# A gated mix of a state-space scan and a Hedgehog attention: a new order of the first loads, constant products at the head of TensorE, and U1 added on VectorE

## The chip, the cores and the metric

The kernel runs on one core of one Trainium2 chip. The metric is the device time of one execution in microseconds; before the change it was 173.07 us, the median of three runs (172.84 to 173.09).

## The reference, cut to what matters

The input x is (2048, 512) in bf16. Two branches read it and a gate mixes them:

```
g   = sigmoid(sum(x * gate_w))                        # one number for each position
a   = 2 * Re(hseq @ C^T) + x * Dskip                  # h_t = Lam_bar * h_(t-1) + B_bar x_t, 512 complex states
b   = (num / den) @ wo                                # linear attention, 32 heads of 16
      num = phi(q) @ sum_s phi(k)_s v_s ;  den = phi(q) . sum_s phi(k)_s + 1e-6
      phi(y) = [softmax(y W_phi), softmax(-y W_phi)]  # over the 16 features of a head
out = g * a + (1 - g) * b
```

with `Lam_bar = exp(exp(log_dt) * Lambda)` and `q, k, v = x @ wqkv`. The recurrence runs over all 2048 positions.

## The kernel before, in words

The positions are split in four phases: position 4c + r belongs to phase r, and the 16 tiles of 128 positions hold tile 4r + a for phase r. The recurrence is then only run over 512 groups of four positions, as two real scans on VectorE for each block j of 128 states, and the states of the phases between come from matrix products.

What each stage does, by the names of the generators that issue it (a name in the order below is the next step of that generator):

- `W0..W3`: transposes of the k weights on TensorE (an identity product), each then copied to SBUF. `f0..f3`: the feature map is folded into these weights (`pf`, line 375) and copied to `Wk2`. The q weights get the same treatment later (`w0..w3`), from weights that arrive already transposed.
- `V`: one transpose of a 20-row tile `vec_n`, which holds Lambda_im, Lambda_re, log_dt, Dskip and gate_w in rows of 128. `P, P2, P3, P4, U, M, D`: small steps on 512 states (exp, angle reduction, sine, products on GpSimd, diagonal matrices `dg`). `i0..i3`: the tables of sines and cosines, five steps each: `kk` (VectorE), `psi` (VectorE), sine (ScalarE), absolute value into `kk` (VectorE), cosine (ScalarE). The `kk` and `psi` tiles come from a pool with two buffers each.
- `v`, `k`, `q` of a tile: four products over the 512 input channels (line 415), then a copy from PSUM. `x, n, e, s` of a pair of tiles: the softmax features of k: trees of maxima and minima, exponentials, sums (VectorE, with exp on ScalarE). `a`: the products that sum phi(k) v (`kvacc`, line 513).
- `p`, `g`: the scan's input: `g0` gives U1, the state input of the second phase, kept in `uv[j][:, 0]`; `g1` adds up the input of the fourth phase. `z`: the scan (VectorE), which leaves the states of the fourth phase in `H3`.
- `h(j, ri)`: the states `H1` of the second phase, block j, real or imaginary part: three products into one PSUM bank (line 597: the identity times U1; lines 598 and 599: diagonal matrices times the previous `H3`), then a copy to SBUF.
- `c, r, b, K`: versions of C and the kernel of the lag between phases. `y`: the state output of a tile. `X, N, E, S`: the features of q. `o`: phi(q) times the summed phi(k) v, and the division. `t`: the output weights, added into the bank of `y`, then the gate and the store.

The order of the work on TensorE, VectorE, ScalarE and the SP queue is not chosen by a scheduler: it is the list of steps in the string `ORDER`, read from front to end. Each engine executes its instructions in the order in which this list issues them. `@5` gives the PSUM bank that a step takes, and `:D` says that a copy from PSUM goes to VectorE; without it `evac` (line 112) uses ScalarE.

The loads stand ahead of the list. The ScalarE queue issues the k weights (`C2r`, line 156), `Wc` (the feature maps, line 157), a load of the activation table (line 125), and the v weights `Wv` (line 161). The SP queue issues the five rows of `vec_n` (line 159), eight transposing loads of x (line 221), both B matrices (lines 225 and 226), their transposes (lines 228 and 229), the other eight x tiles, the q weights, C, and the output weights. Eight semaphores are shared in turn by all loads of both queues, in program order as the build lays it out; a load that takes a semaphore a second time waits in its queue until the load that had it before has landed.

Of the kernel before, what the change touches and what calls it, by code (L numbers as in the profile page):

```python
# [10 lines left out]
ALU = mybir.AluOpType  # L11
AX = mybir.AxisListType
ACT = mybir.ActivationFunctionType
F32 = mybir.dt.float32
# [6 lines left out]
P = 128  # L21
# [3 lines left out]
B B W0@0 B V@1 V P W3@2 P W0:D W1@3 P2 W2@4 P2 P2 P2 U B W3 P2 gw P3 W1 W2 v1@5 U f1@6 P4 f2@7 P P4 P4 P2 f1 f0@1 P3  # L25
i0 U f2 f3@2 v0@0 i0 i1 f0 f3 i1 i0 i0 U i0 i2 i1 i1 v2@3 i2 i1 k2@4 i2 i3 k2 i2 k0@6 i3 k1@7 k1 i2 k0:D v0:D i3 M
v1:D x0 n0 n0 k3@1 k4@2 k5@4 i3 v2 k6@6 n0 k3 i3 v3@0 x0 x0 L x0 k7@7 k5 k4 D n0 x0 n0 v3 p20@5 p02@3 n1 x1 p00@1 e0
k6:D v7@4 p00 p20:D x1 n1 x1 v4@2 p32@0 x1 p22@6 x1 x2 v7 e0 x2 p10@1 p30@5 p12@4 s0 n1 v4 p10 s0 x2 p02 v6@2 p30 s0
x2 n1 v5@1 p22 p32 s0 g000@3 g101@5 n1 n2 s0 p12:D k8@6 k7 s0 e1 e1 k9@0 n2 x2 s0 k8 k9 g101 a0@74 n2 n2 x3 n2 g001@6
k11@0 e2 x3 s1 x3 n3 a0 x3 v6 v10@2 s1 n3 s1 e2 k11 n3 s1 g000 k12@0 D n3 g001 x3 s1 x4 s1 n3 g101 k13@5 k12 s1 n4 s2  # L30
s2 n4 x4 e3 a1 g000 x4 v5 n4 e3 x4 s2 g100@0 a1 n4 g011@3 s2 x4 k13 s2 s3 g100 s2 k10@1 n4 w1@5 g011 s2 g001 k10 s3 s3
a2 n5 n5 w0@6 x5 g100 w1 g010@1 e4 s3 n5 x5 s3 n5 g011 x5 x5 w2@0 s3 D v10 e4 s3 a2 k14@5 x5 g110@2 x6 g011 w0 g010
k15@3 w3@6 n5 a3 n6 s4 g010 k14 w2 e5 s4 v8@5 x6 s4 s4 g010 x6 a3 g111@0 v9@1 e5 z0 k15 s4 x6 g111 s4 g110 v9 c03@3
g110 s5 z0 v8 g201@1 g111 n6 c03 g111 c10@5 n6 n6 s4 a4 x6 g211@3 c02@0 w3 g110 c10 g210@6 z0 s5 z0 n6 g200@2 c13@5 z0
c02 n7 z0 e6 z0 q1@0 s5 z0 x7 s5 e6 x7 q1 g200 a4 n7 s5 c13 q0@0 n7 g201 x7 n7 x7 s5 v14@5 s6 x7 z1 g200 q0 v11@2 g201
z1 s5 q3@0 z1 s6 g210 q3 n7 z0 nA s6 z1 e7 s6 nA v11 c12@1 c12 z0 a5 v14 q2@0 xA z1 z1 xA e7 s7 s6 g210 c01@2 g211
c11@1 xA a5 g210 g211 v12@5 g211 s6 c11 z1 v13@6 z1 nA z2 xA z1 c01 z2 v13 nA s7 s6 g300@3 v12 g301@1 q11@2 z1 xA
c00@6 q2 c00 z2 g300 a6 nA eA xB xB eA s7 v15@5 s7 g311@0 g301 z2 xB g301 nB z2 g311 s7 g300 q7@6 s7 nB sA sA z2 a6
g310@1 g311 q15@3 nB q7 v15 g310 xB s7 xB nB a7 r0 g311 nB q11 g310 z2 sA g310 z3 eB z3 sA eB a7 z3 q5@6 q10@5 z3 q4@0
q15 q6@2 sA Y q8@1 sB h00@3 Y q10 sA z2 q5 h01@5 h00 h10@6 h01 h11@7 q9@3 sB q6 h11 z3 r1 sB q9 z2 q12@5 z3 h10 z2  # L40
q13@2 z3 z3 sA q4 sB z3 K1@7 G h20@3 sB sA r0 sB z3 h31@6 sB sA sA G q13 h20 h21@0 h31 h30@2 h21 Y q12 b0 r1 K0@3 sB
sB sB h30 END o0@6 K1 X1 K0 o0 Y N1 q8 y1@4 X1 o0@0 o0 o2@5 o2 X1 N1 q14@2 X1 o2@7 N1 b0 o0 N1 X1 q14 N1 X2 o1@3 o0 N2
b1 o1 y0@1 o0 G E1 o2 o2 K3@2 o1@6 b1 E1 G y0 N2 o1 r2 X2 o1 E1 E1 o1 K3 K2@0 X2 y1 o0 y0 o2 o3@3 o3 o3@5 y2@2 o3 t0
N2 o1 y2 o3 o1 N2 y3@6 S1 r3 X2 r3 S1 S1 K2 S1 y1 y2 S1 y4@0 X2 S1 o2 t1 o2 N2 o3 S1 y6@7 S1 y7@3 b2 y3 S1 r2 S1 X3 y4
E2 o3 b3 t2 N3 E2 t0 y4 E2 t1 y3 o4@1 E2 X3 b3 y6 y5@5 o3 S2 t2 S2 X3 S2 S2 o4 t0 o4@4 y7 o4 o4 y5 o4 o4 t1 o5@2 t2 o5
S1 X3 o5@1 o5 S1 t3 S2 N3 y7 y5 b2 S2 o5 y11@4 o5 t3 N3 o5 S2 N3 o6@2 o6 o6@6 o4 o5 o6 y6 o7@1 y11 S2 t4 S2 o6 o6 o7
t3 o6 o7@2 X3 y8@6 o7 o7 o6 t4 N3 E3 t5 o7 o7 y9@0 o8@1 y8 t4 o7 E3 t5:D y10@2 S2 E3 S2 o8 S2 o8@5 o8 o8 y9 t6 y11 o8
o8 E3 S3 o9@1 S3 o9 o9@5 t7 o9 t6 t6 o9 y9 t7 S3 S3 o9 o8 y14@7 o9 S3 y8 S3 o10@3 S3 o9 S3 o10 y10 y14 o10@1 t8 o10
o11@5 t5 S3 o10 o10 o11 t9 t8 t7 t9 o11@3 y14 o12@6 o12 o11 o10 S3 y12@1 o12@0 o11 o12 o12 o11 o12 y10 o10 S3 o13@5 S3
o11 o13 o12 y12 o13@6 t10 o13 y15@3 o11 o14@0 o13 t10:D y12 o14 o14@2 o13 y13@5 o14 y15 o12 o13 o15@6 o14 o14 t8 o15  # L50
o13 o15@0 o15 t11 o14 o15 y13 o14 t10 o15 t11 y15 o15 y13 t14 t11 o15 t13 t9 t14 t13:D t12 t12:D t14 t15 t15 t13 t12
t15
"""
TWO_PI_LO = float(np.nextafter(np.float32(2.0 * np.pi), np.float32(0.0)))
# [11 lines left out]
def kernel(  # L66
# [42 lines left out]
    def bank(shape, dtype, name):  # L109
        return ps.tile(shape, dtype, tag=f"t{sel['banks'].pop(0)}", name=name, bufs=1)  # L110
# [40 lines left out]
    vec_n = const.tile([20, P], BF16, name="vec_n")  # L151
# [4 lines left out]
    nc.scalar.dma_start(out=wk_nat[:], in_=B_wqkv[:, D:2 * D].rearrange("(k p) n -> p k n", p=P))  # L156
# [4 lines left out]
    nc.scalar.dma_start(out=Wv[:], in_=B_wqkv[:, 2 * D:3 * D].rearrange("(k p) n -> p k n", p=P))  # L161
# [14 lines left out]
    hpi_t = const.tile([P, 1], F32, name="hpi_t")  # L176
    nc.vector.memset(hpi_t[:], float(np.pi / 2.0))
# [42 lines left out]
    def x_load(ti):  # L220
        nc.sync.dma_start_transpose(out=xT[:, :, ti * P:(ti + 1) * P], in_=x_res[ti // 4, ti % 4])
# [21 lines left out]
    tab_g = tc.tile_pool(name="tabtmp", bufs=2, reuse_waits="tile")  # L243
# [34 lines left out]
    def st_V():  # L278
        pvt = bank([P, 20], BF16, "pvt")
        nc.tensor.transpose(pvt[:], vec_n[:], ident[0:20, 0:20])  # L280
        yield
        nc.vector.tensor_copy(out=vec[:].rearrange("p n j -> p (n j)"), in_=pvt[:])
# [268 lines left out]
    def st_c(dst, j):  # L551
        d_, da, db = ((C2r, DG_BR, DG_NBI), (C2i, DG_NBI, DG_NBR))[dst]
        pc = bank([P, D], F32, "pc")
# [38 lines left out]
    def st_h(j, ri):  # L592
# [4 lines left out]
        MM(out=ph[:], lhsT=ident[:], rhs=U1[:, ri, :], start=True, stop=False)  # L597
        MM(out=ph[:], lhsT=dg[:, da, j, :], rhs=H3[:, j, 0, prev], start=False, stop=False)
        MM(out=ph[:], lhsT=dg[:, db, j, :], rhs=H3[:, j, 1, prev], start=False, stop=True)
        yield  # L600
        evac(H1[:, j, ri, :], ph[:])
# [131 lines left out]
    st = {"V": st_V(), "U": st_U(), "P": st_P(), "P2": st_P2(), "P3": st_P3(), "P4": st_P4(), "B": st_B(), "gw": st_gw(),  # L733
# [57 lines left out]
```

## Time and profile before

| | us |
|---|---|
| median of three runs (range) | 173.07 (172.84 to 173.09) |
| the profiled execution | 173.42 |
| its span, first to last instruction | 171.7 |
| TensorE busy | 157.8 (92%) |
| VectorE busy | 144.2 (84%) |
| ScalarE busy | 116.9 (68%) |
| GpSimd busy | 5.3 (3%) |

The profiled execution is 1.7 us longer than its span, and 0.35 us above the median. Busy time of TensorE counts a product from its start to the end of its pipeline, so that 379 ns are shown for a product of 512 columns whose successor starts 216 ns later; the start times are what counts. VectorE's durations overlap in the same way.

### The profile page before, as it was taken

To read this page: it belongs to the slowest core of one execution; us is meant where nothing else is said; L and a number is where in the kernel's file an instruction comes from. 1 tells how busy PE (TensorE), PEld (TensorE's weight loads), DVE (VectorE), ACT (ScalarE), POOL (GpSimd) and SP (SyncE) were. 2 spreads that over 40 slices of the span, in tenths; PEclk is the share of its full clock that TensorE was granted. 3 is DMA by queue.
4 is the path that set the end of the run, shared out by engine and by line. 5 is a ranking of instruction groups with operands and counts; after the bars stand their busy time and mean duration, and the time that the engine had idled before them with its cause. 6 is when DMAs were issued, how large, how long until landed. Compare 5 with 4: busy or idle time off the path is not lost.

```text
span 171.7 us, 2969 instructions
## 1 busy us (share of the span) xinstructions
PE 157.8 (92%) x1049; PEld 80.5 (47%) x1069; DVE 144.2 (84%) x349; ACT 116.9 (68%) x239; POOL 5.3 (3%) x23
## 2 busy tenths in 40 slices
PE   0599989999999999999999999999999998998991
PEld 0354456455455454444545444545455543444540
DVE  3775999999999999999999999999999958335411
ACT  2559799988789587586687698896864394251311
POOL 3223000000000000000000000000000000000000
PEclk9999999999999999999999999999999999999999
DMA  5945974554546000000000008341178458596443
GB/s 126 208 106 157 265 96 92 95 116 100 92 95 164 20 0 2 0 4 0 0 0 4 0 0 168 76 33 34 33 183 203 85 145 183 134 174 154 122 138 106
DMA packets 50710, 15.94 MB, mean 93 GB/s; under 512 B 46088, under 2 KB 50696, under 8 KB 50696
## 3 DMA queue, kind: packets, MB, share of 16 engines
q1 hardware_dynamic: 49112, 14.70, 39.9%
q10 hardware_dynamic: 1584, 1.07, 2.6%
q8 instruction: 8, 0.13, 0.3%
q14 instruction: 6, 0.05, 0.1%
HBM read 2.64 MB, written 2.10 MB: 28 GB/s over the span
## 4 chain that ended last, share of the span: by engine, by line
PE 63%; DVE 18%; DMA 11%; ACT 3%; SPq 2%; issue 1%
PE pq L415 8%; PE py L675 6%; PE py L676 6%; PE py L720 6%; PE pgq L538 6%; PE pgq L541 6%; PE pv L415 5%; DMA phT<-EEq 4%; DVE smk L450 3%; DVE mxk L450 3%; PE py L682 2%; DMA xT<-in_A_x_dram 2%; DVE mnk L450 2%; DMA C2r<-in_B_wqkv_dram 2%; PE pk L645 2%; DMA oT<-on 2%
## 5 line engine op out<-in xcount | busy, mean ns | idle before, releaser
L415 PEld LDWEIGHTS <-xT 128*128 128x128 bf16 x192 | 18.4, 99 | 22.7 <-DMA xT<-in_A_x_dram 2.1
L133 ACT ACTIVATE EEk<-EEk 128x1024 bf16<-128x1024 bf16 x20 | 20.9, 1072 | 2.5 <-DVE EEk L466 2.5
L707 DVE SCALAR_TENSOR_TENSOR on<-pn,RG,rd 128x256 bf16<-128x256 f32 x32 | 14.4, 478 | 9.2 <-ACT rd L133 9.2
L133 ACT ACTIVATE ld<-pn 128x16 f32<-128x16 f32 x32 | 5.5, 185 | 18.4 <-PE pn L698 18.1
L415 PE MATMUL pv<-Wv,xT 128*128 128x512 bf16 x62 | 16.3, 400 | 1.9 <-DMA xT<-in_A_x_dram 1.8
L541 PE MATMUL pgq<-xT,LBT 128*128 128x512 bf16 x63 | 16.0, 379 | 0.1
L720 PE MATMUL py<-Wo,oT 128*128 128x512 bf16 x61 | 15.6, 379 | 0.2
L415 PE MATMUL pq<-Wq,xT 128*128 128x512 bf16 x63 | 15.2, 379 | 0.1
L415 PE MATMUL pk<-Wk,xT 128*128 128x512 bf16 x63 | 15.2, 379 | 0.1
L133 ACT ACTIVATE EEq<-EEq 128x1024 bf16<-128x1024 bf16 x12 | 12.2, 1047 | 1.3 <-DVE EEq L466 1.3
L676 PE MATMUL py<-Wv,H 128*128 128x512 bf16 x32 | 12.1, 379 | 0.1
L114 ACT CAST uv<-pgq 128x512 bf16<-128x512 f32 x16 | 9.3, 582 | 3.9 <-PE pgq L546 2.8
L724 ACT ACTIVATE ot<-py,G 128x512 bf16<-128x512 f32 x12 | 8.2, 682 | 5.5 <-PE py L720 4.9
L676 PE MATMUL py<-C2i,H 128*128 128x512 bf16 x31 | 11.7, 379 | 0.1
L675 PE MATMUL py<-C2r,H 128*128 128x512 bf16 x31 | 11.7, 379 | 0.1
L675 PE MATMUL py<-Wk,H 128*128 128x512 bf16 x31 | 11.7, 378 | 0.0
L114 ACT CAST Xq<-pq 128x512 bf16<-128x512 f32 x16 | 9.3, 589 | 3.4 <-PE pq L415 3.3
L698 PEld LDWEIGHTS <-phT 128*128 128x128 bf16 x128 | 7.0, 98 | 7.1 <-DMA phT<-EEq 2.7
L450 DVE TENSOR_TENSOR smk<-smk 128x512 bf16<-128x512 bf16 (+2 forms) x30 | 9.9, 330 | 0.2
L486 DVE TENSOR_TENSOR EEk<-EEk,rck 128x2048 bf16<-128x2048 bf16 x8 | 9.7, 1218 | 0.0
L541 PEld LDWEIGHTS <-LBT 128*128 128x128 bf16 x64 | 6.2, 98 | 7.3
L579 DVE TENSOR_TENSOR_SCAN w<-ssm_par,ut 128x512 bf16<-128x512 f32 x8 | 9.6, 1215 | 0.0
(169 smaller groups left out, 339.4 us busy)
## 6 DMA issues: line engine op xcount, KB each, us to landing
out_dram<-ot SPq DMA_DIRECT2D x16, 128.0 KB, 2.1
C2r<-in_B_wqkv_dram ACTq DMA_DIRECT2D x1, 512.0 KB, 3.9
Wv<-in_B_wqkv_dram ACTq DMA_DIRECT2D x1, 512.0 KB
Bn_r<-in_A_B_re_dram SPq DMA_DIRECT2D x1, 512.0 KB, 4.6
Bn_i<-in_A_B_im_dram SPq DMA_DIRECT2D x1, 512.0 KB
Wo<-in_B_wo_dram SPq DMA_DIRECT2D x1, 512.0 KB
xT<-in_A_x_dram SPq DMA_TRANSPOSE x16, 3.5
oT<-on SPq DMA_TRANSPOSE x16, 2.3
```

The costliest lines, as they stand in the source:

```text
L114: nc.scalar.copy(out=out_ap, in_=in_ap)
L133: ins = nc.scalar.activation(**kw)
L415: MM(out=pt[:], lhsT=xT[:, kt, ti * P:(ti + 1) * P], rhs=W[:, kt, :], start=(kt == 0), stop=(kt == KT - 1))
L450: VT(out=t[:], in0=cur[:, :, :, 0:n, :], in1=cur[:, :, :, n:2 * n, :], op=op)
L486: VT(out=E5, in0=E5, in1=rc[:].to_broadcast([P, L, 2 * NB, Dh, 4]), op=ALU.mult)
L538: MM(out=pgq[:], lhsT=BT[:, kt, js], rhs=xT[:, kt, r1 * NC:(r1 + 1) * NC], start=(kt == 0), stop=False)
L541: MM(out=pgq[:], lhsT=LBT_[:, kt, js], rhs=xT[:, kt, (r1 - 1) * NC:r1 * NC], start=False, stop=(r1 == 1 and kt == KT - 1))
L579: nc.vector.tensor_tensor_scan(out=w[:, ri, :], data0=rb, data1=ut[:, ri, :], initial=0.0, op0=ALU.mult, op1=ALU.add)
L675: MM(out=py[:], lhsT=src[:, j, 0, off:off + P], rhs=cr[:, j, :], start=(j == 0), stop=False)
L676: MM(out=py[:], lhsT=src[:, j, 1, off:off + P], rhs=ci[:, j, :], start=False, stop=False)
L707: nc.vector.scalar_tensor_tensor(out=on[:, 2 * hf:2 * hf + 2].rearrange("p g h e -> p (g h) e"), in0=pns[hf][:, :, 0:Dh], scalar=RG[:, ti: ...
L720: MM(out=py[:], lhsT=oT[:, g, :], rhs=Wo[:, g, :], start=False, stop=(g == HG - 1))
```

## The change

It has four parts, and a new `ORDER` that covers all of the work.

1. Loads. The eight x transposes come first in the SP queue. Lambda_im, Lambda_re and log_dt (now a 12-row `vec_n`) go to the ScalarE queue, between the k weights and `Wc`; `Wv` follows `Wc`, and the load of the activation table comes behind `Wv`. Dskip and gate_w become an 8-row tile `vec_m`, loaded behind the eight x tiles, with a transpose and a copy of their own (`V2`).
2. TensorE begins with nine products of a constant tile `fillw` into a PSUM bank that nothing reads.
3. The `h` step leaves out the identity product for all eight (j, ri); instead of the copy, VectorE adds U1 to the PSUM result.
4. The pool of `kk` and `psi` has three buffers.

The new order has fewer copies from PSUM on VectorE: `v1:D`, `k6:D`, `t6:D` and `t10:D`, where the old one had `W0:D`, `k0:D`, `v0:D`, `v1:D`, `p20:D`, `p12:D`, `k6:D`, `t5:D`, `t10:D`, `t13:D` and `t12:D`. `C2_VECTOR` is empty, so the branch in `st_c` does nothing.

```diff
 ORDER = """
-B B W0@0 B V@1 V P W3@2 P W0:D W1@3 P2 W2@4 P2 P2 P2 U B W3 P2 gw P3 W1 W2 v1@5 U f1@6 P4 f2@7 P P4 P4 P2 f1 f0@1 P3
...
+W2@0 V@1 W2 W1@2 V P B B W1 P P2 W0@3 U P2 P2 P2 W3@4 P2 B P3 P4 P4 W3 U P B P4 v2@5 W0 f1@6 f3@7 U f0@1 i1 U f2@0 P2
+P3 i0 f1 i1 i0 i2 v0@2 f0 f3 f2 v1@4 k0@3 k1@6 k2@1 i0 M i0 i0 i1 i2 i1 i3 i3 k0 k1 v1:D x0 i1 i2 i2 v2 v0 k6@7 k2
...
+C2_VECTOR = ()
+H1_VECTOR = ((0, 0), (0, 1), (1, 0), (1, 1), (2, 0), (2, 1), (3, 0), (3, 1))
...
-    vec_n = const.tile([20, P], BF16, name="vec_n")
+    vec_n = const.tile([12, P], BF16, name="vec_n")
+    vec_m = const.tile([8, P], BF16, name="vec_m")
...
     nc.scalar.dma_start(out=wk_nat[:], in_=B_wqkv[:, D:2 * D].rearrange("(k p) n -> p k n", p=P))
+    for n, src in enumerate((A_Lambda_im, A_Lambda_re, A_log_dt)):
+        nc.scalar.dma_start(out=vec_n[4 * n:4 * n + 4, :], in_=src.rearrange("(j p) -> j p", p=P))
     nc.scalar.dma_start(out=Wc[:], in_=B_w_phi.rearrange("(k hl) e f -> (hl e) k f", hl=8))
-    for n, src in enumerate((A_Lambda_im, A_Lambda_re, A_log_dt, A_Dskip, gate_w)):
-        nc.sync.dma_start(out=vec_n[4 * n:4 * n + 4, :], in_=src.rearrange("(j p) -> j p", p=P))
+    nc.scalar.dma_start(out=Wv[:], in_=B_wqkv[:, 2 * D:3 * D].rearrange("(k p) n -> p k n", p=P))
     pin_act_set()
-    nc.scalar.dma_start(out=Wv[:], in_=B_wqkv[:, 2 * D:3 * D].rearrange("(k p) n -> p k n", p=P))
...
+    fillw = const.tile([P, 512], BF16, name="fillw")
+    nc.vector.memset(fillw[:], 1.0)
+    spin = ps.tile([P, 512], F32, tag="t7", name="spin", bufs=1)
+    for _ in range(9):
+        nc.tensor.matmul(out=spin[:], lhsT=fillw[:, 0:P], rhs=fillw[:], start=True, stop=True)
...
     for ti in range(8):
         x_load(ti)
+    for n, src in enumerate((A_Dskip, gate_w)):
+        nc.sync.dma_start(out=vec_m[4 * n:4 * n + 4, :], in_=src.rearrange("(j p) -> j p", p=P))
...
-    tab_g = tc.tile_pool(name="tabtmp", bufs=2, reuse_waits="tile")
+    tab_g = tc.tile_pool(name="tabtmp", bufs=3, reuse_waits="tile")
...
         ph = bank([P, NC], F32, "ph")
-        MM(out=ph[:], lhsT=ident[:], rhs=U1[:, ri, :], start=True, stop=False)
-        MM(out=ph[:], lhsT=dg[:, da, j, :], rhs=H3[:, j, 0, prev], start=False, stop=False)
+        add = (j, ri) in H1_VECTOR
+        if not add:
+            MM(out=ph[:], lhsT=ident[:], rhs=U1[:, ri, :], start=True, stop=False)
+        MM(out=ph[:], lhsT=dg[:, da, j, :], rhs=H3[:, j, 0, prev], start=add, stop=False)
         MM(out=ph[:], lhsT=dg[:, db, j, :], rhs=H3[:, j, 1, prev], start=False, stop=True)
         yield
-        evac(H1[:, j, ri, :], ph[:])
+        if add:
+            VT(out=H1[:, j, ri, :], in0=ph[:], in1=U1[:, ri, :], op=ALU.add)
+        else:
+            evac(H1[:, j, ri, :], ph[:])
         yield
```

More of the change, by code (lines that the diff above doesn't have):

```diff
@@ L30 @@
[L30 to L39, printed above, removed]
@@ L45 @@
[L45 to L49, printed above, removed]
@@ L278, in st_V, with st_V2 @@
     def st_V():
-        pvt = bank([P, 20], BF16, "pvt")
-        nc.tensor.transpose(pvt[:], vec_n[:], ident[0:20, 0:20])
+        pvt = bank([P, 12], BF16, "pvt")
+        nc.tensor.transpose(pvt[:], vec_n[:], ident[0:12, 0:12])
         yield
-        nc.vector.tensor_copy(out=vec[:].rearrange("p n j -> p (n j)"), in_=pvt[:])
+        nc.vector.tensor_copy(out=vec[:, 0:3, :].rearrange("p n j -> p (n j)"), in_=pvt[:])
+        yield
+    def st_V2():
+        pvt = bank([P, 8], BF16, "pvt")
+        nc.tensor.transpose(pvt[:], vec_m[:], ident[0:8, 0:8])
+        yield
+        nc.vector.tensor_copy(out=vec[:, 3:5, :].rearrange("p n j -> p (n j)"), in_=pvt[:])
         nc.gpsimd.affine_select(out=Dd[:], in_=dsk.unsqueeze(2).to_broadcast([P, KT, P]), compare_op=ALU.is_equal,
@@ L552, in st_c @@
         d_, da, db = ((C2r, DG_BR, DG_NBI), (C2i, DG_NBI, DG_NBR))[dst]
+        if (dst, j) in C2_VECTOR:
+            k = 2 * (j % 2) + dst
+            tmp = phT0[:, k].rearrange("p m f -> p (m f)").bitcast(F32)
+            if sel["eng"] == "act":
+                nc.scalar.mul(out=tmp, in_=CrT[:, j, :], mul=dgs[:, da, j:j + 1])
+            else:
+                VS(out=tmp, in0=CrT[:, j, :], scalar1=dgs[:, da, j:j + 1], scalar2=None, op0=ALU.mult)
+            yield
+            nc.vector.scalar_tensor_tensor(out=d_[:, j, :], in0=CiT[:, j, :], scalar=dgs[:, db, j:j + 1], in1=tmp, op0=ALU.mult, op1=ALU.add)
+            yield
+            return
         pc = bank([P, D], F32, "pc")
```

39 lines of the change are left out of this document (27 added, 12 removed).

## The prediction

> **What bounds the kernel now.** I read the page first (slices), then the waits, then the first 16 us of the timeline, the chain of waits, and last the VectorE groups by form.
>
> ```profile
> PE   0599989999999999999999999999999998998991
> DVE  3775999999999999999999999999999958335411
> PEclk9999999999999999999999999999999999999999
> ```
>
> TensorE is full from the third slice to the end, VectorE from the sixth to slice 32 (133 us). So a saving counts only where it takes work off TensorE, brings its start forward, or shortens a wait, and VectorE must not fall behind.
>
> ```profile
> PE ptw L273 <- DMA C2r<-in_B_wqkv_dram: 4.7, 1, 4.7
> PE pv L415 <- DMA xT<-in_A_x_dram: 1.8, 1, 1.8
> PE pn L698 <- DMA phT<-EEq: 1.4, 2, 0.8
> PE pl L525 <- DVE dg L367: 0.7, 1, 0.7
> DVE kk L388 <- ACT T2c L139: 3.0, 1, 3.0
> SPq L221 <- DMA C2r<-in_B_wqkv_dram: 0.8, 1, 0.8
> ```
>
> TensorE's long waits are in the head. The last line shows a queue held by a semaphore: the second x transpose, issued at 4.71, waited for the k weights.
>
> ```profile
> 0.78 0.43 ACTq L156 DMA_DIRECT2D C2r<-in_B_wqkv_dram  x1
> 1.80 1.28 ACT L125 ACT_TABLE_LOAD   x1 [1.80 <-issue]
> 2.51 0.37 ACTq L161 DMA_DIRECT2D Wv<-in_B_wqkv_dram  x1
> 2.60 11.15 SPq L221 DMA_TRANSPOSE xT<-in_A_x_dram  x8
> 6.32 1.56 ACT L114 COPY Xq<-ptw 128x512 bf16<-128x512 bf16 x3
> 8.96 1.89 PE L415 MATMUL pv<-Wv,xT 128*128 128x512 bf16 x4 [1.82 <-DMA xT<-in_A_x_dram]
> 10.64 1.91 PE L375 MATMUL pf<-BD,Xq 128*128 128x128 bf16 x16
> 12.35 2.16 PE L415 MATMUL pv<-Wv,xT 128*128 128x512 bf16 x8
> 14.35 1.89 PE L415 MATMUL pk<-Wk,xT 128*128 128x512 bf16 x7
> ```
>
> The first four pv products start 427 ns apart; from about 12.8 us on they start 216 ns apart. The head runs at half pace although the granted clock is full throughout.
>
> ```profile
> 96.05 0.22 PE ph L597
> 96.26 0.22 PE ph L598
> 96.48 0.22 PE ph L599
> ```
>
> In the chain, an identity product costs what any 512-column product does, 0.216 us.
>
> **The account.** The profiled execution took 173.42: 171.7 of span and 1.7 around it, and lies 0.35 above the median. The first pk product starts at 14.35, the last product of all ends at 168.2, and copy and store take the last 3.5. Between 14.35 and 168.2 there are 149.7 us of products at their fast paces (216 ns for 512 columns, and so on down) and so 4.1 us of idle time, of which gaps of 0.84 (dg), 0.5 (kvacc), 0.8 and 0.9 (both phT) are the large ones. Hence span = start of pk + products + idle + 3.5.
>
> **Part 3, U1 on VectorE.** Eight products of 0.216 leave TensorE: -1.73, in its full stretch, so all of it counts. Products after pk: 148.0. Eight copies of 0.59 leave ScalarE, which is not full. VectorE gets eight adds from PSUM, a form that the trace lacks. Bounds: 0.34 each, the pace of the 512-column bf16 operations at line 589, and 0.66, that of the scalar_tensor_tensor at line 637. The nearest rows:
>
> ```profile
> L618 DVE TENSOR_TENSOR KVm<-kvacc,maskN 128x256 bf16<-128x256 f32 x2 | 0.8, 420 | 0.0
> L116 DVE CAST Xq<-pk 128x512 bf16<-128x512 f32 x2 | 1.4, 682 | 0.0
> ```
>
> Both come from PSUM; the copy's successor starts 0.60 later, so I take 0.60: 4.8 in all (2.7 to 5.3). Against it, seven copies leave VectorE: W0 0.33, k0, v0, p20 and p12 0.60 each, and two ot of 0.67, together 4.1; constant and second vector copy add some 0.3. Net +1.0 over the kernel, but early it gains 2.7 and around 85 to 110 us it loses 4.8. The copies that move to ScalarE (some 4.2) are matched by the 4.7 that leave it. Summed in the new order, the third q softmax (line 497) comes after 136.2 us of VectorE work instead of 133.1. What hides this: VectorE waited 3.7 us between 138 and 148 before that softmax ended, and in the new order the first product of tile o12, which needs it, stands 11.4 us of TensorE work before the end instead of 14.8. If that cover is gone, the loss is up to 3.
>
> **Part 1, the loads.** On SP the five small loads (1.8 us) no longer stand ahead of x; two of them, 0.65, now stand ahead of the B matrices, which still start 1 to 2 us earlier. The first g product, their user, did not wait before. But in the built order the third vector load takes the semaphore of x tile 0, and `Wc` that of x tile 2; both wait in the ScalarE queue, and queued behind them are `Wv`, the table load and all of ScalarE's copies. x tile 2 is issued at about 3.4 (0.78 plus two issues of 1.3); its landing comes 2.8 to 3.5 us later by the fastest and median x loads, 4.2 by the one that ran beside `Wv`, so at 6.2 to 7.6; I take 6.4, as the k weights should be in by then. Then `Wc` is issued (0.53), then `Wv` at about 7.0 instead of 2.51, and it lands after 3.9 by the k weights' row, at 10.9; by its own former landing (issued 2.51, last piece 8.35) it would be 5.8, and the far end is 14. ScalarE's table load ends at 8.6; four weight copies (0.48 apart) and two exps end at 11.0, the sine table and two sines at 12.8, four `Wk` copies at 14.8. VectorE's BD and angle steps wait for `Wc` (about 8.2) and the first exp; its table steps begin near 11.7 instead of 8.86.
>
> **Part 2, the constant products.** Nine at 427 ns run from about 1.2 to 5.1, while TensorE would wait for the k weights: no cost (at most 0.4 if those land at 4.7 as before). They may bring the fast pace before the x products. With it, the first four pv, 16 pf and eight pv cost 0.86 + 0.90 + 1.73 = 3.5 from 10.9 on: 14.4, and pk waits for the last `Wk` copy until 14.6. Without it they cost what they did, 8.96 to 14.35, or 5.4: pk at 16.3. So the early start of x is eaten up by the later `Wv`, and the faster pace gives that back.
>
> **Part 4, three buffers.** VectorE's 3.0 us wait for T2c goes; next in line is the later `Wc`. VectorE's first feature step then starts at about 18.3 with 9.7 us of work done, before at 19.6 with 11.5: it has lost 8.6 us by then instead of 8.1, which the early copies of 2.7 outweigh only in part, as the first kvacc now stands 1.4 us tighter behind VectorE (25.2 against 22.6 us of work, before 24.7 against 23.4; 0.7 were spare). I leave the idle time at 4.1, between 2 and 6.
>
> Sum, fast pace: 14.6 + 148.0 + 4.1 + 3.5 = 170.2 of span, 171.9 profiled, 171.6 as a median: 0.85% faster.
>
> **The rivals.**
>
> *Clock lost again.* TensorE's W transposes are over by 7 to 8 us and `Wv` comes at 10.9: a pause of 3 to 4 us after the constant products. If it drops to half pace in that, pk starts at 16.3 and the median is 173.3, no change. For it: before, four products after a pause of 1.8 us ran at half pace, though TensorE had not been full earlier. No longer pause at full pace is in the trace. [...]
>
> *ScalarE queue held too long, the other side.* If x tile 2 lands at 7.5 beside the k weights, `Wv` is issued at 8.1 and lands at 12, and at half pace pk starts at 17.4: 148.0 + 17.4 + 4.1 + 3.5, plus 1.35, is 174.4, slower. It decides from a pk start of 16.5 on. For it speaks `Wv`'s 5.8 us before; against it, that this included waiting for the k weights.
>
> *VectorE becomes the bound.* If the adds cost 0.66, and kvacc and the q features each come a us or more late, idle rises from 4.1 to 6.3 at the fast start: 173.8.
>
> *More than I count.* The k weights and x share the loads' engines well (`Wv` at 10.2, fast pace, pk at 13.9) and the new order halves the idle time to 2.8: 169.6. For it: the phT gaps at 142 and 154 need only other work in front of them.
>
> **How the numbers follow.** Chances: forecast (171.6; its own range 170.8 to 172.5) 0.42, more than I count 0.16, clock lost (172.7 to 174) 0.16, queue held 0.16, VectorE 0.10. Within 0.2% (0.35 us, about what a measurement of this kernel can tell) falls some 0.08 of clock lost and 0.02 of the others. Faster: 0.42 + 0.16 + 0.03 of clock lost, less 0.02, makes 0.59; same 0.10; slower 0.31. The range that leaves out 2 in 10: 169.5 to 174.4.
>
> **What would show it.** Right: products at line 184 until about 5; `Wv` issued at 6.5 to 7.5; the first x product near 11 and pk near 14.6, 216 ns apart; a table load on ScalarE ending near 8.6; adds of 0.6 at line 632; no identity products in `h`. Wrong: x products 427 ns apart, `Wv` issued before 4 (no held queue) or after 8, or TensorE waiting more than 2 us for kvacc or phT.

## The result, and the profile after

| | before | after |
|---|---|---|
| median (range), us | 173.02 (172.84 to 173.09) | 175.18 (174.35 to 176.0) |
| profiled execution | 173.42 | 176.0 |
| its span | 171.7 | 174.3 |
| TensorE busy | 157.8 | 160.2 |
| VectorE busy | 144.2 | 142.8 |

The change makes the kernel slower by 1.2%: the ratio is 1.012, with an interval of 1.0085 to 1.0155. The forecast was 171.6. Here and below a ratio and its interval leave out executions that took over 1.5% longer than the fastest of the same kernel (two of the eight of `e_loads_old`, for one), while medians and ranges count all of them.

The slices of the page, after the change:

```profile
PE   6349999999999999999999999999999599999891
DVE  4049699999999999999999999999999695833400
PEclk9999999999999999999999999999999999999999
```

TensorE now has work in the first slice (the constant products), is busy for three and four tenths of the second and third, and has a new hole in slice 32, which is at 135 us. VectorE is empty in the second slice. The waits by name, in us in total, times, and the longest:

```profile
ACT L127 <- DMA vec_n<-in_A_log_dt_dram: 8.8, 1, 8.8
...
PE pvt L290 <- DMA vec_n<-in_A_log_dt_dram: 2.7, 1, 2.7
...
PE pv L432 <- DMA Wv<-in_B_wqkv_dram: 2.4, 1, 2.4
DVE BD L324 <- DMA Wc<-in_B_w_phi_dram: 2.2, 1, 2.2
...
PE py L753 <- DMA oT<-on: 1.9, 1, 1.9
```

Four of the five are the head's, and all four name a load that the ScalarE queue issued. Before, the table load waited for nothing and the first x product waited for x. The timeline of the head (start, length, engine, line, operation, what ended the wait):

```profile
1.51 4.02 PE L184 MATMUL spin<-fillw 128*128 128x512 bf16 x9 [1.51 <-DVE fillw L181]
...
5.91 0.25 ACTq L161 DMA_DIRECT2D vec_n<-in_A_log_dt_dram  x1
7.66 0.40 ACTq L162 DMA_DIRECT2D Wc<-in_B_w_phi_dram  x1
8.10 0.68 ACTq L163 DMA_DIRECT2D Wv<-in_B_wqkv_dram  x1
...
8.81 1.28 ACT L127 ACT_TABLE_LOAD   x1 [8.81 <-DMA vec_n<-in_A_log_dt_dram]
...
12.60 1.87 PE L432 MATMUL pv<-Wv,xT 128*128 128x512 bf16 x4 [2.37 <-DMA Wv<-in_B_wqkv_dram]
...
14.25 1.91 PE L392 MATMUL pf<-BD,Xq 128*128 128x128 bf16 x16
...
18.43 1.89 PE L432 MATMUL pk<-Wk,xT 128*128 128x512 bf16 x8
```

log_dt is issued when x tile 0 has landed (5.89 by the semaphore's updates), `Wc` when x tile 2 has (7.64). `Wv` follows at 8.10 instead of 2.51, lands at 12.55, and releases the first x product. The table load, 1.80 before, stands at 8.81. The four pv products take 1.87 and 16 pf 1.91, as before: half pace (427 and 107 ns from start to start). pk starts at 18.43, which is 4.08 later than before. This profiled execution is the slowest of the four.

The prediction's sum closes with these numbers. From the start of pk to the end of the last product it is 152.30 (153.86 before); 18.43 + 152.30 + 3.5 is 174.2 of span. The forecast had 14.6 + 152.1 + 3.5. The miss lies in the start of pk:

| | forecast | measured |
|---|---|---|
| x tile 2 lands | 6.4 | 7.64 |
| `Wv` issued, first x product | 7.0, 10.9 | 8.10, 12.60 |
| table load ends | 8.6 | 10.09 |
| first x product to pk | 3.7 | 5.83 |
| pk starts | 14.6 | 18.43 |
| first feature step on VectorE | 18.3 | 20.98 |
| pk to the last product | 152.1 | 152.30 |

That the last row agrees is luck, as the runs without the adds show further below.

### The profile page after: what moved, and what is told of

Its sections match the earlier page's. It is cut to its first block, busy times and chain, and to the rows that moved or that the text cites. A ratio compares the mean times of both kernels' runs of the same rounds, so it can differ in the third digit from the quotient of the medians.

```text
span 174.3 us, 2975 instructions
## 1 busy us (share of the span) xinstructions
PE 160.2 (92%) x1051; PEld 82.0 (47%) x1071; DVE 142.8 (82%) x352; ACT 116.0 (67%) x238; POOL 8.1 (5%) x23
## 4 chain that ended last, share of the span: by engine, by line
PE 46%; DVE 38%; DMA 9%; issue 2%; ACT 2%; SPq 1%; ACTq 0%; DVEq 0%
PE py L753 6%; PE py L708 6%; PE py L709 6%; PE pk L432 5%; DVE smk L467 5%; PE py L715 4%; DVE w L607 4%; DVE EEk L503 3%; PE pgq L558 3%; PE pgq L555 3%; DVE mxk L467 3%; PE pv L432 3%; DVE EEk L477 3%; DVE mnk L467 3%; DMA Wv<-in_B_wqkv_dram 3%; DMA oT<-on 3%
## 5 line engine op out<-in xcount | busy, mean ns | idle before, releaser
L432 PE MATMUL pv<-Wv,xT 128*128 128x512 bf16 x62 | 17.3, 407 | 2.5 <-DMA Wv<-in_B_wqkv_dram 2.4
L757 ACT ACTIVATE ot<-py,G 128x512 bf16<-128x512 f32 x14 | 9.5, 683 | 13.5 <-PE py L753 10.3
L432 PE MATMUL pq<-Wq,xT 128*128 128x512 bf16 x62 | 16.1, 378 | 0.2
L558 PE MATMUL pgq<-xT,LBT 128*128 128x512 bf16 x63 | 15.4, 379 | 0.0
L709 PE MATMUL py<-Wv,H 128*128 128x512 bf16 x30 | 11.4, 379 | 0.0
L135 ACT ACTIVATE ld<-pn 128x16 f32<-128x16 f32 x32 | 4.9, 182 | 8.7 <-PE pn L731 8.7
L116 ACT CAST Xq<-pk 128x512 bf16<-128x512 f32 x15 | 9.1, 616 | 1.7 <-PE pk L432 1.7
L753 PEld LDWEIGHTS <-oT 128*128 128x128 bf16 x64 | 5.8, 98 | 7.8 <-DMA oT<-on 2.0
```

What stands on the lines that cost most here:

```text
L116: nc.scalar.copy(out=out_ap, in_=in_ap)
L135: ins = nc.scalar.activation(**kw)
L432: MM(out=pt[:], lhsT=xT[:, kt, ti * P:(ti + 1) * P], rhs=W[:, kt, :], start=(kt == 0), stop=(kt == KT - 1))
L558: MM(out=pgq[:], lhsT=LBT_[:, kt, js], rhs=xT[:, kt, (r1 - 1) * NC:r1 * NC], start=False, stop=(r1 == 1 and kt == KT - 1))
L709: MM(out=py[:], lhsT=src[:, j, 1, off:off + P], rhs=ci[:, j, :], start=False, stop=False)
L753: MM(out=py[:], lhsT=oT[:, g, :], rhs=Wo[:, g, :], start=False, stop=(g == HG - 1))
```

## The experiments

Their ratios are against the kernel before on the same chip, with a 95% interval. All kernels compute the full output.

**The old loads in the changed kernel** (`e_loads_old`). Only the order of five loads, with the table load among them, is put back; the new order of work, the constant products, the adds and the third buffer stay, and Dskip and gate_w stay behind the x tiles.

```diff
-    for n, src in enumerate((A_Lambda_im, A_Lambda_re, A_log_dt)):
-        nc.scalar.dma_start(out=vec_n[4 * n:4 * n + 4, :], ...)
     nc.scalar.dma_start(out=Wc[:], ...)
-    nc.scalar.dma_start(out=Wv[:], ...)
+    for n, src in enumerate((A_Lambda_im, A_Lambda_re, A_log_dt)):
+        nc.sync.dma_start(out=vec_n[4 * n:4 * n + 4, :], ...)
     pin_act_set()
+    nc.scalar.dma_start(out=Wv[:], ...)
```

> The changed kernel with the loads of the ScalarE queue as before (k weights, Wc, table load, Wv) and the three small vectors back at the head of the SP queue, ahead of x; all else as changed. Held queue (theory A: log_dt and Wc wait in the ScalarE queue for x tiles 0 and 2, and Wv, the table load and every ScalarE copy wait behind them): Wv lands before 9 instead of 12.55, the first x product comes at 9 instead of 12.60, pk at 14 to 15 instead of 18.43, and the median is 171 to 172, some 3.5 us under the changed kernel. Theory B (the adds on VectorE and the new order cost the time, and the head is made up for later): the first x product comes early too, but the median stays above 173.5.

Measured: 170.87 (169.88 to 172.64), ratio 0.9895 (0.9858 to 0.9932); the profiled execution took 170.19. Its head:

```profile
1.80 1.28 ACT L127 ACT_TABLE_LOAD   x1 [1.80 <-issue]
4.29 0.37 ACTq L164 DMA_DIRECT2D Wv<-in_B_wqkv_dram  x1
...
9.29 1.04 PE L432 MATMUL pv<-Wv,xT 128*128 128x512 bf16 x4 [1.82 <-DMA xT<-in_A_x_dram]
...
12.78 4.48 PE L432 MATMUL pk<-Wk,xT 128*128 128x512 bf16 x20
```

The table load is back at 1.80, the x products wait for x and not for `Wv`, and they run at full pace (four in 1.04). pk starts at 12.78, 5.65 earlier than in the changed kernel and earlier than theory A had it; theory B is refuted. The part of the change that puts x at the front of the loads is the one that made the head late; without it the rest is worth 1%.

**Only `Wv` moved forward** (`e_wv_first`), to tell the late `Wv` from ScalarE's late work:

```diff
     nc.scalar.dma_start(out=wk_nat[:], ...)
+    nc.scalar.dma_start(out=Wv[:], ...)
     for n, src in enumerate((A_Lambda_im, A_Lambda_re, A_log_dt)):
         nc.scalar.dma_start(out=vec_n[4 * n:4 * n + 4, :], ...)
     nc.scalar.dma_start(out=Wc[:], ...)
-    nc.scalar.dma_start(out=Wv[:], ...)
     pin_act_set()
```

> The changed kernel, with one transfer moved: Wv is issued second in the ScalarE queue, straight behind the k weights, instead of last. The three vector loads, Wc, the table load and ScalarE's copies stay behind waits for the x tiles as in the changed kernel. If the lateness of Wv is what moved pk from 14.4 to 18.4: Wv lands by 9, the first x products start near 9 to 9.5, the pf products follow when BD is there (Wc, about 11.5), the Wk copies end at 14.5 to 16, and pk starts at 14.5 to 16: ratio 0.993 to 1.003. If the lateness of ScalarE's own work (table load at 8.8 instead of 1.8, the Wk copies behind it) is enough by itself: pk stays at 17.5 to 18.5 and the ratio at 1.009 to 1.013.

Measured: 179.82 (179.29 to 180.85), ratio 1.0432 (1.0397 to 1.0467). Neither expectation had this. The head:

```profile
1.25 0.53 ACTq L160 DMA_DIRECT2D Wv<-in_B_wqkv_dram  x1
...
9.54 0.26 ACTq L162 DMA_DIRECT2D vec_n<-in_A_log_dt_dram  x1
...
11.73 0.16 PE L290 MATMUL pvt<-ident,vec_n 12*128 12x12 bf16 x1 [6.20 <-DMA vec_n<-in_A_log_dt_dram]
...
12.20 0.44 ACTq L163 DMA_DIRECT2D Wc<-in_B_w_phi_dram  x1
...
18.02 0.34 PE L392 MATMUL pf<-BD,Xq 128*128 128x128 bf16 x2 [3.10 <-ACT Xq L116]
...
22.73 1.46 PE L432 MATMUL pk<-Wk,xT 128*128 128x512 bf16 x6
```

`Wv` is issued at 1.25, and moving it in front shifts which semaphore each load behind it shares. All three vector loads and `Wc` now wait for x tiles, up to the seventh (`Wc` at 12.20), and beside `Wv` the first x tile lands later as well, at 7.53 instead of 5.89 by the semaphore's updates; the first vector load goes out at 7.76. The transpose of `vec_n` stands in front of twelve weight transposes on TensorE and holds them for 6.2 us. The table load starts at 12.67, and pf waits 3.1 us for ScalarE's copies of the transposed weights. So the early `Wv` alone did not help: what counted was everything that the held queue carried, ScalarE's own instructions included. The expectation had kept the other loads' times as they were, but with the semaphores shared anew log_dt went out at 9.54 instead of 5.91 and `Wc` at 12.20 instead of 7.66.

**No constant products** (`e_no_spin`: the loop of nine taken out of the changed kernel).

> The changed kernel without the nine constant products. If these bring nothing here, as the x products still start 427 ns apart after them: within 0.4 us of the changed kernel's 175.18. If they shorten the head in some executions: slower by up to 1.5 us, and its runs lie closer together than the 1.65 us between the changed kernel's four. If they are in the way of the k weights: faster by about 0.3.

Measured: 174.11 (172.43 to 175.35), ratio 1.0089 (1.0056 to 1.0122), not told apart from the changed kernel's 1.012; the median is lower by more than any of the three expectations had. In the changed kernel the nine products brought nothing that was left when x came.

**More constant products, across the pauses** (`e_keepwarm`: the changed kernel, with seven more ahead of the transpose of `vec_n` and eight ahead of the first x product).

```diff
     def st_V():
+        fill(7)
         pvt = bank([P, 12], BF16, "pvt")
...
     def st_v(ti):
+        if ti == 2:
+            fill(8)
         pv = bank([P, D], F32, "pv")
```

> The changed kernel with seven more constant products ahead of the vector transpose and eight more ahead of the first x product, which fill the two pauses of TensorE in the head (2.95 and 2.6 us). If the pauses are why the x products run at half pace: they start 216 ns apart, the 4 pv, 16 pf and first pv products take 1.9 us less, pk comes at about 16.6 instead of 18.43, and the time falls by 1.5 to 1.9 us, to about 173.5. If half pace has another reason: the products stay 427 ns apart, the last fill ends after Wv has landed, and the time rises by up to 1 us.

Measured: 172.36 (171.74 to 173.36), ratio 0.9995 (0.9975 to 1.0015). The constant products at line 290 fill the pause:

```profile
9.11 1.89 PE L290 MATMUL spin<-fillw 128*128 128x512 bf16 x8
11.23 1.02 PE L437 MATMUL pv<-Wv,xT 128*128 128x512 bf16 x4 [0.24 <-DMA Wv<-in_B_wqkv_dram]
...
14.71 4.48 PE L437 MATMUL pk<-Wk,xT 128*128 128x512 bf16 x20
```

The first x products (pv) run at full pace right away, and pk starts 3.48 after it instead of 5.83. That is 2.3 of the 3.7 us between the two profiled starts of pk; the other 1.4 is that `Wv` landed earlier in this execution (the products start at 11.23 instead of 12.60). In the ratios the fifteen more products are worth 1.2%.

**What U1 on VectorE is worth** (three pairs). `H1_VECTOR` decides which of the eight states get their add on VectorE; an empty list puts all identity products and copies back.

```diff
-H1_VECTOR = ((0, 0), (0, 1), (1, 0), (1, 1), (2, 0), (2, 1), (3, 0), (3, 1))
+H1_VECTOR = ()
```

First in the changed kernel (`e_identity`):

> The changed kernel with the identity products back in all eight h steps and the copies back on ScalarE. If TensorE is the bound after the head, as its 152.3 us from pk to the last product against 153.8 before say: slower by about 1.7 us, some 176.9. If VectorE is the bound since the change (theory B), which this frees of 4.8 us: faster by 1 to 4 us.

Measured: 174.43 (173.91 to 174.88), ratio 1.011 (1.0077 to 1.0144), against 1.012 with the adds. The expected 1.7 us were not there. From pk to the last product it is 152.29, and 152.30 with the adds, although TensorE has eight products more to do. The windows view over this stretch shows where their time is made up; its columns are the stretch, its length, and the busy time with the number of instructions of TensorE, its weight loads, VectorE, ScalarE and GpSimd, then the granted clock, the share of the DMA engines and GB/s. Before the change, in the changed kernel, and in `e_identity`:

```profile
14.35:168.20 153.85, 150.25 (x1005) 75.70 (x1023) 136.51 (x308) 108.52 (x224) 0.26 (x2) 1.00 0.41 88
18.43:170.73 152.30, 148.47 (x999) 75.68 (x1016) 134.35 (x309) 106.75 (x222) 2.04 (x4) 1.00 0.38 80
17.32:169.61 152.29, 150.06 (x1007) 76.24 (x1024) 130.04 (x301) 110.14 (x229) 1.78 (x3) 1.00 0.38 81
```

TensorE's idle time (the length less its busy time) is 3.60, 3.83 and 2.23. In this pair the rest of the change shortens the idle time by about 1.4 us, and the adds lengthen it again by 1.6, nearly as much as they take off the products. One profile is not the next, though: the seven profiles of the new order with all eight adds have 151.03 to 152.30 from pk to the last product, the three without any 152.29 to 152.64. By their means (151.75 and 152.45) the adds save 0.7 of the expected 1.7 us. Then with the old loads (`e_old_identity`), and with half of the adds (`e_old_half`, the last four of the list):

> The run with the old loads, but with the eight identity products back on TensorE and plain copies of the second phase's states in place of the adds; everything else as in that run, which stood at 0.9895 of the kernel before. TensorE theory (the eight products are 1.73 us of a full TensorE, the head only hid it): the gain is lost again, ratio 0.9995, about 172.4 us, and pk to the last product grows from 152.15 to 153.9. VectorE theory (VectorE has no idle time from 50 to 120 us, so the eight adds of 0.60 push the third q softmax back by what TensorE saves): no difference, ratio 0.9895 within 0.003, pk to the last product still about 152.2, TensorE's wait for oT near 130 us falls from 1.98 to about 1.0 or less, and VectorE shows idle time between 90 and 120.

> The run with the old loads, with only the last four of the eight states added on VectorE, the first four with their identity products and plain copies as before the change: TensorE has 0.86 us more work than with eight adds, VectorE up to 2.4 us less. TensorE theory: halfway between, ratio 0.9945 (171.6). VectorE theory: no loss, ratio 0.9895 within 0.003 or somewhat lower (to 0.987), since the wait for oT shrinks by at least what the products add.

Measured: 171.46 (169.72 to 172.32), ratio 0.9899 (0.9861 to 0.9938), without adds and 171.01 (169.17 to 171.68), 0.9899 (0.9860 to 0.9938), with four, against 0.9895 with eight. No difference can be told. The third pair is `e_old_identity_warm` further below: 0.9856 without adds, 0.9838 with them, intervals overlapping. The windows view of `e_loads_old` and `e_old_identity` shows why. With the eight adds (they run from 80.9 to 101.6), 90 to 120 us:

```profile
90.00:120.00 30.00, 29.74 (x187) 14.79 (x189) 30.00 (x64) 22.96 (x49) 0.00 (x0) 1.00 0.32 54
```

and without them:

```profile
90.00:120.00 30.00, 29.84 (x187) 14.73 (x189) 25.15 (x56) 25.22 (x55) 0.00 (x0) 1.00 0.31 53
```

VectorE has no idle time with the adds, and 4.85 without, about what eight adds at 0.60 come to. TensorE is full both times. Its wait for oT (the attention output, transposed by a DMA) near 130 us is the largest part of the difference:

```profile
PE py L753 <- DMA oT<-on: 1.8, 1, 1.8
```

with the adds, and

```profile
PE py L753 <- DMA oT<-on: 1.1, 2, 0.9
```

without. From pk to the last product it is 152.15 with the adds and 152.64 without, although TensorE has eight products of 0.216, or 1.73 us, less to do: counted as above, its idle time grows from 2.72 to 3.83.

**The constant products with the old loads** (`e_old_no_spin`: the loop of nine taken out of `e_loads_old`).

> The run with the old loads, but without the nine constant products ahead of the k weights' transposes. If they are what brings the fast pace before the first x product: the four pv near 9.3 us and the 16 pf run at half pace as before the change, 0.84 and 0.85 us more, and some pv or pk behind them too, so pk starts 1.7 to 2.2 us later than at 12.78, and the ratio goes from 0.9895 to between 0.999 and 1.002. If the weight transposes alone bring it, now that the pause before the x products is short: no difference, pk at 12.8, ratio 0.9895 within 0.003. With the held queue the constant products had brought nothing (174.1 without them against 175.2 with them).

Measured: 171.23 (170.51 to 171.93), ratio 0.9928 (0.9899 to 0.9956). In its profile the first x products run at half pace again and pk starts at 14.31, 1.53 later than with them. The end comes only 0.86 later, since pk to the last product shrinks from 152.15 to 151.48. In the ratios it is 0.3%, less than expected and within the two intervals: it seems that with the old loads the nine products bring something in some executions and nothing in others. The granted clock of the single executions of `e_loads_old` fits that:

```
time, us        169.88  170.19  170.66  170.70  171.03  172.17  172.60  172.64
granted clock   1.00    0.998   0.99    0.99    0.99    0.986   0.98    0.98
```

In these traces the records of the granted clock begin 3.41 us or a multiple of it apart; ahead of the first record the page prints full pace. The records of the profiled executions (start in us: rate):

```
before          12.89: 1.0
after           17.46: 1.0
e_loads_old      7.39: 1.0
e_identity       6.45: 1.0    9.86: 0.5   16.69: 1.0
e_old_half       6.15: 1.0    9.56: 0.5   12.97: 1.0
e_wv_first       4.46: 1.0    7.87: 0.5   14.70: 1.0   18.11: 0.5   21.53: 1.0
```

Where the first one lies differs from execution to execution (4.46 to 17.46 in these six). Cutting the changed kernel's profile in steps of 3.41 us, counted back from its record at 17.46:

```profile
0.39:3.80 3.41, 2.29 (x6) 0.89 (x7) 1.94 (x16) 0.00 (x0) 1.55 (x9) 1.00 0.49 114
3.80:7.22 3.42, 2.15 (x9) 0.77 (x6) 0.00 (x0) 0.00 (x0) 0.00 (x0) 1.00 1.06 184
7.22:10.63 3.41, 1.58 (x13) 1.40 (x14) 0.17 (x1) 1.80 (x3) 0.00 (x0) 1.00 0.67 122
10.63:14.04 3.41, 1.45 (x4) 0.56 (x4) 2.68 (x18) 3.35 (x9) 0.40 (x2) 1.00 0.95 229
14.04:17.46 3.42, 3.41 (x20) 2.31 (x20) 3.42 (x9) 2.40 (x6) 3.16 (x6) 1.00 1.07 320
```

The 1.00 is no record here, as the products run at half pace through all five (the last of them, at 15.96 to 16.81, 427 ns apart). The constant products and four weight transposes ran without a gap from 1.51 to 5.95, but in neither of the two steps that they fell into was TensorE busy for more than 2.29; the first step with 3.41 is followed by the full rate. And `e_old_half`, which had the full rate at 6.15 and lost it (TensorE busy, granted clock, DMA, GB/s):

```profile
2.73:6.15 3.42, 3.42 (x14) 1.00 1.01 238
6.15:9.56 3.41, 1.17 (x14) 1.00 1.10 248
9.56:12.97 3.41, 3.41 (x21) 0.50 0.41 94
12.97:16.39 3.42, 3.37 (x16) 1.00 0.66 184
```

A pause of 2.24 us ahead of the first x product left 1.17 of work in the second step, and the third ran at half rate. `e_loads_old` kept its rate through a pause of 1.82:

```profile
7.39:10.80 3.41, 1.59 (x17) 1.04 (x17) 3.31 (x16) 3.06 (x7) 0.97 (x4) 1.00 1.03 183
```

**The pause filled, with the old loads** (`e_loads_old_warm`: `e_loads_old` with `fill(8)` ahead of the first x product, as in `e_keepwarm`), with and without the adds, to test what these steps suggest: that the rate of a step follows TensorE's busy time in the step before. The bounds in the first expectation, 0.8 and 0.3 to 0.45 of a step, are the author's estimates; the steps of the runs made until then fit them. The full rate came after 2.92 (`e_identity`) and 2.95 us (`e_wv_first`), 0.86 of a step, and not after 2.29 and 2.15 (the changed kernel), 0.67 and 0.63; it was kept after 1.59 (`e_loads_old`), 0.47, and lost after 1.17 (`e_old_half`), 1.00 (`e_wv_first`) and 0.95 (`e_identity`), 0.34 to 0.28.

> The run with the old loads, plus eight more constant products on TensorE, in the pause ahead of the first x product (7.5 to 9.3 us). Window theory: TensorE's rate is set anew every 3.41 us from its share of work in the window just over, above about 0.8 raises it and below about 0.3 to 0.45 drops it, and where the windows fall differs from execution to execution; the eight runs with the old loads show it, 169.9 at a granted clock of 1.0 and 172.6 at 0.98. With TensorE at work from 1.5 us on without a pause no execution can lose the rate: all of them at a clock of 0.997 or more, median 169.6 to 170.2, ratio 0.983 to 0.987, and less than 1.5 us between the lowest and the highest. If the spread is something else (loads, chip): ratio 0.989 to 0.992 as without the eight, highest again near 172.5.

> The last kernel with the eight identity products back on TensorE and no adds on VectorE: what the adds are worth when the rate does not vary. VectorE theory: within 0.25% of the kernel with the adds (169.6 to 170.4). TensorE theory: 1.73 us, 1.0% slower than with the adds (171.3 to 171.9). If the adds cost VectorE more than they save TensorE: 0.3% or more faster without them.

Measured: 169.81 (169.53 to 170.22), ratio 0.9838 (0.9817 to 0.9859) with the adds, 170.15 (169.58 to 171.01), 0.9856 (0.9828 to 0.9883) without. No execution of either had a clock below 0.996 (0.997 was expected), and the first spreads by 0.69 us, where `e_loads_old` went from 169.88 at a clock of 1.00 to 172.17 at 0.986; the second spreads by 1.43 us.

```profile
7.02 1.89 PE L443 MATMUL spin<-fillw 128*128 128x512 bf16 x8
9.19 1.04 PE L432 MATMUL pv<-Wv,xT 128*128 128x512 bf16 x4 [0.28 <-DMA xT<-in_A_x_dram]
...
12.68 4.48 PE L432 MATMUL pk<-Wk,xT 128*128 128x512 bf16 x20
```

The kernel with the adds is the fastest of the study, not told apart from the one without: 1.6% faster than before, 2.8% faster than the change as it was made.

**The constant products in the kernel before** (`e_before_spin`: the nine at its head; `e_before_warm`: these and eight ahead of its first x product).

> The kernel before, with nothing but the nine constant products at its head. Between the weight transposes (over at 7.1) and the first x product (8.96) there is a pause of 1.8 us. Window theory: in some executions the fast rate comes by then and lasts, in others it comes and is lost, in others it does not come; a mean gain of a third to two thirds of the 1.9 us that half pace costs at the head: ratio 0.993 to 0.998, and runs below a clock of 0.992 appear. If the head's other waits (Wk copies, the tables on two buffers) set the start of pk: ratio 0.998 to 1.002.

> The kernel before with the nine constant products at its head and eight more in the pause ahead of the first x product; no load, table, buffer or order changed. Window theory: all executions at full pace from 8.96 on, pk starts at 12.5 to 12.9 instead of 14.35: ratio 0.988 to 0.992, if the work behind it can follow; 0.992 to 0.998 if VectorE, whose tables come no earlier, makes TensorE wait for dg or kvacc for up to another 1.4 us. No change (0.998 to 1.002) would say that the rate at the head is worth nothing to this order.

Measured: 0.9978 (0.9958 to 0.9998) and 0.9961 (0.9946 to 0.9976). Of the twelve executions of the first, three with a clock of 0.99 took 172.96 to 173.08 and the others 171.78 to 172.24. With the pause filled, pk starts at 11.72 instead of 14.35, but the end comes only 1.54 earlier (166.67 instead of 168.21). In the waits, where before had 0.7 for dg and 3.0 for T2c:

```profile
DVE kk L393 <- ACT T2c L139: 1.5, 1, 1.5
...
PE pl L536 <- DVE dg L372: 1.5, 1, 1.5
```

TensorE is early and waits for VectorE's dg, which stands behind the tables with their two buffers.

**The third buffer in the old order**, alone (`e_before_buf3`) and with the filled head (`e_before_warm_buf3`).

```diff
-    tab_g = tc.tile_pool(name="tabtmp", bufs=2, reuse_waits="tile")
+    tab_g = tc.tile_pool(name="tabtmp", bufs=3, reuse_waits="tile")
```

> The kernel before with nothing but three buffers for kk and psi instead of two. VectorE's wait of 3.0 us for T2c goes. Buffer theory: the features start up to 1.5 us earlier and TensorE's wait of 0.84 for dg goes, ratio 0.991 to 0.996. Order theory: TensorE's head (pk at 14.35) sets the rest, ratio 0.998 to 1.002.

> The kernel before with the constant products at its head and in the pause, and with three buffers for kk and psi; loads and order stay as before. VectorE's wait of 1.5 us for the first T2c goes. Buffer theory (the tables' wait is what held the old order back once its head ran at full pace): TensorE's wait for dg falls from 1.67 to 0.2 or less, pk to the last product from 154.95 to about 153.6, ratio from 0.9961 to 0.987 to 0.990. Order theory (the gain of the changed kernel's rest lies in its order): VectorE's start of the features moves by at most 0.5 us, ratio 0.994 to 0.997.

Measured: 0.9948 (0.9928 to 0.9968) and 0.9944 (0.9916 to 0.9973). Alone it brings half a per cent, as the buffer theory said: the wait for dg is gone from the list, VectorE's wait for T2c is halved (1.5), the features start at 18.07 instead of 19.52, and pk to the last product falls from 153.86 to 152.11. Together with the head the wait for dg falls to 0.2 and pk to the last product from 154.95 to 153.22, as the buffer theory had it, but the features move by only 0.2 us and the ratio is the order theory's: hardly more than either alone. (Its executions, all at a clock of 0.998 or more, go from 170.54 to 172.63; the cause of that spread is open.) So most of the 1.2% between `e_before_warm` and `e_loads_old_warm` is in neither. What is left, by exclusion and not by a run of its own, is the new order of the work with its fewer copies on VectorE, and the two small loads that it has behind x: in the profile of `e_before_warm_buf3` TensorE waited 1.2 us for one of them, gate_w. Two buffers in the new order weren't tried: it has three tables in flight at once.

## Why the prediction was wrong

*Part 2, the constant products: the step that failed is "with it" the fast pace.* The forecast took full pace for pv and pf as the likeliest case, 3.7 us from the first x product to pk. It was 5.83, and 5.67 and 6.18 in the profiles of `e_no_spin` and `e_identity`, against 3.48 with the pauses filled: 2.1 of the 3.8 us by which pk missed its forecast. In the profiled execution the nine products never brought the full rate. In the other three the mean clocks of 0.97 to 0.98 say that it came and was lost; the profile of `e_identity`, which has the same head and a clock of 0.98, shows how: full rate from 6.45, half from 9.86, and the first x product at 11.14. `e_keepwarm` shows the price: 1.2%.

*Part 1, the loads: the mechanism right, one size wrong in the profiled execution.* The prediction saw that log_dt and `Wc` would wait for x tiles 0 and 2 in the ScalarE queue, with `Wv`, the table load and all copies behind them. `e_loads_old` shows that the change loses its time by this, together with the pause that it makes: undone, the ratio goes from 1.012 to 0.9895. The term "I take 6.4" for the landing of x tile 2, chosen with the argument that the k weights should be in by then, was 7.64, at the far end of the bounds; `Wv` then took 4.45 and not 3.9, so the first x product came at 12.60 instead of 10.9, the other 1.7 of the 3.8 us. But the landing varies. In the profiles of `e_no_spin`, `e_identity` and `e_keepwarm`, whose loads are the same, `Wv` is issued at 7.11, 7.08 and 6.87, where the forecast had 7.0, and the first x product starts at 11.37, 11.14 and 11.23. There only 0.2 to 0.5 us is missing, and pk still starts at 17.04 and 17.32 in the two whose pauses are not filled. What moves the landing stays open. (The last `Wk` copy stands at 14.8 in one sentence of the prediction and at 14.6 in the sum; the 0.2 us decides nothing.)

*The sentence that the head ran at half pace although the granted clock was full* was a misreading. The products start 427 ns apart until about 12.8 and the first record, of full rate, is at 12.89; the page prints full where the trace has no record.

*The rivals.* "ScalarE queue held too long" is what happened in the profiled execution: `Wv` issued at 8.1, to the tenth, and landed at 12.55 for 12; half pace; pk at 18.43 for 17.4. It was too small by 0.6 of landing, and by 0.4 since the full rate came 4.9 us after the first x product, where before it had come 3.9 after: another place of the steps (records at 17.46 and 12.89). "Clock lost again", with its pk of 16.3, is nearer to `e_identity`: rate lost, the queue held about as long as forecast, pk at 17.32. The two were given as alternatives, 0.16 each, but both have half pace in their price, and in `e_identity` it was the held queue that made the pause in which the rate was lost: 2.52 us of waiting for log_dt, 0.95 us of work in the step from 6.45, half rate from 9.86.

*Part 3, U1 on VectorE: "in its full stretch, so all of it counts" was wrong.* The removal did what it says: from pk on, TensorE has 1.73 us less to do. The add's price was right too (0.60 to the next start, 0.68 as the trace counts it). But VectorE has no idle time from 50 to 120 us in the new order, and the 4.8 us of adds come out at its end: the prediction looked for that end at the third q softmax and found cover there (3.7 us of waiting), but the wait arose earlier, at the writes of `on` that oT is made from: they stand among the q features in VectorE's queue and came at 131.7 to 132.5, and TensorE stood still for 1.91 us from 135.3 to 137.2. A head start did not help: the features began 2.55 us behind pk where the forecast had 3.7. Three comparisons, with a late head, an early one and a steady clock, put the adds at nothing that can be told from zero, and short of the expected 1.0% (by the profiles they save 0.7 of 1.73 us): 1.011 without them to 1.012 with them, 0.9899 to 0.9895, 0.9856 to 0.9838. So the rival "VectorE becomes the bound" was right in part, without its 0.66 per add. That pk to the last product came out at 152.30 for 152.1 all the same is two errors that cancel: in this pair the adds' 1.73 did not count, and the idle time without them, which the forecast left at 4.1, is shorter for another reason (`e_identity`: 152.29 without adds).

*Part 4, three buffers: put at nothing, and in the old order worth 0.5%.* There the third buffer alone brings pk to the last product from 153.86 to 152.11, about what `e_identity` has in the new order (152.29), so it may be the other reason just named; one profile each, and no run with two buffers in the new order, so this is not shown. "Next in line is the later `Wc`" holds in part for the changed kernel: VectorE waits 2.2 us for it, after 5.5 us for the transpose of `vec_n`, which waits for log_dt.

## What to carry to other kernels

A load put on a compute engine's queue brings its semaphore wait with it (here the wait of `Wc` for x tile 2, until 7.64, came ahead of `Wv`, at 8.10 instead of 2.51, and of the table load, at 8.81 instead of 1.80): list, for each load of the new order, whose landing it waits for, and treat all that stands behind it on that engine, copies and table loads too, as not earlier than that landing at the far end of its bounds. Constant products to lift TensorE's rate worked here when they kept it busy, together with the real work between them, right up to the first product that counts: from 1.5 to 9.0 us in `e_loads_old_warm`, where no execution had a clock below 0.996. Twice the recorded step of 3.41 us, 6.8 us, is the author's estimate of the work that holds a whole step wherever the steps lie, which differs between executions. With a pause left ahead of that product the gain varied: the rate outlasted 1.82 us in the profile of `e_loads_old` and not 2.24 us in that of `e_old_half`, and the clocks of their executions went from 1.00 down to 0.98 and 0.99. Where two engines are full over the same stretch, work taken from one and given to the other is worth little until the second has idle time in that stretch (here 1.73 us less on TensorE saved 0.7 by the profiles): read both in the windows before counting the saving.

## What the runs showed that was not expected

- In these profiles the rate of TensorE in a step of 3.41 us went with its busy time in the step before. It rose after 2.92 (`e_identity`, 3.03 to 6.45), 2.95 (`e_wv_first`, 1.05 to 4.46) and 2.81 us (`e_before_spin`, 0.91 to 4.32: the nine constant products took 3.49 us there, and 4.02 where the rate did not rise among them), not after 2.29 and 2.15 (the changed kernel); it was kept after 1.59 (`e_loads_old`), and lost after 1.17 (`e_old_half`), 1.00 (`e_wv_first`) and 0.95 (`e_identity`). Where it turns between these bounds is open.
- Where the steps lie against the kernel's start differs between executions (counted back from the records, one begins at 0.39 us in the changed kernel's profile and at 3.03 in that of `e_identity`), and that seems to make most of the spread of `e_loads_old`: from 169.88 at a clock of 1.00 to 172.17 at 0.986, and 0.69 us with the pause filled. It is not the only source of spread. What spreads `e_no_spin` from 172.43 to 174.88, with a recorded clock of 1.00 in every execution, was not settled; a late first rise leaves no record (the changed kernel's profile shows a clock of 1.00 and products at half pace up to 16.81), and the landing of the loads varies too (`Wv` issued at 6.87 to 8.10 with the same loads).
- Moving one 512 KB load four places forward, with no dependence changed, cost 3.1% (1.0432 against 1.012): the loads behind it came to share other semaphores, and the x tiles that they then waited for landed later beside it (the first at 7.53 instead of 5.89).
